# A spectral transformer block's gradient: who copies and stores the w2 gradient, four sets of gz tiles, and three moved pieces of matmul work

## The chip, the cores and the metric

The kernel runs on one core of one Trainium2 chip. The metric is the device time of one execution in microseconds; lower is better. The core's engines are TensorE (PE, matmuls), VectorE (DVE), ScalarE (ACT), GpSimd (POOL) and SyncE (SP, which here only asks for DMAs). Each engine works its own list of instructions in order and waits on semaphores for the others. DMAs are asked for by SyncE and GpSimd.

## The reference

The kernel computes the output and all gradients of one block (`jax.vjp`): 2048 tokens, D = 1024, F = 3584, everything bf16.

```python
mod = (_silu(c) @ w_mod).reshape(1, 6, 1, -1)        # six rows: sa, ca, ga, sb, cb, gb
h = _layernorm(x) * (1 + ca) + sa
x = x + ga * irfft2(rfft2(h) * (w_r + 1j * w_i))      # mixer A, over tokens and channels
h = _layernorm(x) * (1 + cb) + sb
y = _layernorm(h)
x = x + gb * (gelu(y @ w1 + b1) @ w2 + b2)            # mixer B
# and then, from grad_out: the gradients of x, w_r, w_i, w1, b1, w2, b2, c, w_mod
```

The outputs that matter below: `out_1` is the gradient of x, `out_2` and `out_3` those of `w_r` and `w_i`, `out_4` that of w1 (1024 x 3584), `out_6` that of w2 (3584 x 1024), `out_9` that of `w_mod`.

## The kernel before

One long program, not a loop: the language's scheduler orders each engine's list from the program's order, with some priorities (`tc.high_priority()`) and hand-written orders (`tc.issue_after(x)`: this comes behind x on its engine or by a semaphore). Tiles are named by tags; a tile with the tag of an older one lies in its place and waits until that one's last reader is done. PSUM has tags `f` (four accumulators of 128 x 512), `s` (two) and `d` (two).

The stages in order of time:

1. From 0 to some 125 us: the rows of modulation (`pm`, L278), and meanwhile the product of the output gradient with w2^T in blocks of 128 columns: `ph_part(fc, js)`, matmuls `pp` at L813, 8 for each of the four token quarters `js`. Blocks 0 to 5 (`PH_EARLY`) and the first two quarters of block 6 are written ahead of the first spectral part, the rest behind it.
2. The first spectral part (forward of mixer A): `s_fwd` (matmuls `pu`, L537, that read the folded input `fbuf`), channel transforms (`pcs`, L576), the product with `w_r + i w_i`, and back (`pv`, `po`).
3. The MLP forward (`pz`, L949), the output product (`pbo`, L1003), and the gradient with respect to its input: `pg_pass` (L1103), four passes b over the token quarters, each with two halves h of 7 w1^T groups g of 16 matmuls. Behind a pass of quarter b the column sums of quarter b - 1 (`sums3`, matmuls `acc3a` and `acc3b` at L217, that read `gn3a`, `gn3b`, `pru` and `au`, made by VectorE) are put among the groups: behind group 2, 3 and 4.
4. From some 944 us: the second spectral part (backward of mixer A), again `pu`, `pcs`, `pv` (L646, L662) and `po` (L748), with ScalarE copying V out of PSUM (L780). Its gaps on TensorE are filled by a generator, `pieces()`, called as `fill(n)`: n products of the w2 gradient (`gw2acc`, L1236, 16 matmuls each, one half row block of 128 x 512), and after all 56 of those the w1 gradient (`gw1acc`, L1454, 7 groups `fg` of 8 products).
5. The w2-gradient products are copied out by `gw2_out` (L1240 to L1247): into `gwo5` or `gwo[:, fc % 2]` (four halves that turn), by VectorE or ScalarE as the scheduler chooses (`nc.any`), and stored to `out_6`, all by GpSimd; from fc = 8 on half by half (L1245).
6. `consume_bwd(i, ...)`, i = 0 to 3, is the end of the second spectral part: VectorE unfolds a quarter of the result, does the layer norm backward, loads `xt` from `d_gx` (L1383, by SyncE), adds, stores `out_1`, and then TensorE sums columns (`accCA`, L217), with `fill((4, 6, 6, 8)[i])` ahead of that sum and `fill(3 if i == 1 else 2)` behind it.
7. Each w1-gradient group needs its 512 columns of `gz`, transposed on load from `d_gz` by SyncE (`gw1_load`, L1402), 1 MB in each of two tiles. Two sets of two tiles turn: group fg uses set fg % 2, and group fg + 1 is asked for ahead of group fg.
8. To the end, from some 1333 us: the rest of the w1 gradient, beside it rows 2, 1, 0 of the modulation gradient (`gmod_row`: loads `gr` and `wrw` by SyncE, VectorE's products, stores by GpSimd), ordered behind the last `gz` load that has been asked for.

The lists of SyncE and GpSimd matter here: SyncE has, in the stretch of stage 6, the `gz` loads, the `xt` loads and the `out_1` stores in one queue; GpSimd has the `out_6` and `out_9` stores, the stores of `out_2` and `out_3` and the spectral weights' loads in one.

Of the kernel before, what the change touches and what calls it, by code (L numbers as in the profile page):

```python
# [11 lines left out]
BF16 = mybir.dt.bfloat16  # L12
# [5 lines left out]
P = 128  # L18
# [5 lines left out]
NFC = F // P  # L24
# [6 lines left out]
NB = 4  # L31
# [4 lines left out]
def kernel(  # L36
# [24 lines left out]
    nc = tc.nc  # L61
    CE, CO, SE, SO = 0, 1, 2, 3
# [3 lines left out]
    reg = ctx.enter_context(tc.tile_pool(name="reg", bufs=1))  # L66
# [183 lines left out]
    c8, gb2r, b1r = (genv[0:n, 3136 + k * P:3136 + (k + 1) * P] for k, n in enumerate((NDC, NDC, NFC)))  # L250
# [94 lines left out]
    fbuf = reg.tile([P, 4, 4, D], BF16, name="fbuf", tag="fr")  # L345
# [177 lines left out]
    last_pu = [None]  # L523
    last_po = [None]

    def s_fwd(cl, fb, sm, evac):
        Ut = reg.tile([P, 8, 512], BF16, name=f"U{cl}", tag=f"uv{cl}")
        for c8 in range(8):
            pu = (ps_f if cl % 2 == 0 and c8 % 2 and fb is not fbuf else ps_s)("pu")
            for i in range(4 if cl % 2 else 0):  # L530
                last_pu[0] = nc.tensor.matmul(pu[:], lhsT=fb[:, i, cl, c8 * P:(c8 + 1) * P], rhs=sm[:, i, :],
                                              start=(i == 0), stop=(i == 3))
            for k in range(0 if cl % 2 else 2):
                cols = slice(k * 256, (k + 1) * 256)
                for j in range(2):
                    i = 2 * j + (k if cl == CE else 1 - k)
                    last_pu[0] = nc.tensor.matmul(pu[:, cols], lhsT=fb[:, i, cl, c8 * P:(c8 + 1) * P], rhs=sm[:, j, cols],  # L537
                                                  start=(j == 0), stop=(j == 1))
            with tc.high_priority():
                evac(Ut[:, c8, :], pu[:])  # L540
        return Ut
# [261 lines left out]
    last_pe = [None]  # L803
# [4 lines left out]
    def ph_part(fc, js):  # L808
        ph2 = phs[fc % 4]
        for j in js:  # L810
            pp = ps_f("pp")
            for cch in range(NDC):
                last_pe[0] = nc.tensor.matmul(pp[:], lhsT=wt[:, fc % 4, cch, :], rhs=gBoT[j][:, cch, :],  # L813
                                              start=(cch == 0), stop=(cch == NDC - 1))
            q = (0, 2, 3, 1)[j]
            ov = ph2[:, :, q * P:(q + 1) * P]
            pv = pp[:, :].rearrange("p (i w) -> p i w", w=P)
            with tc.high_priority():
                nc.any.tensor_copy(out=ov, in_=pv)  # L819
        if js[-1] == 3:  # L820
            nc.gpsimd.dma_start(out=d_ph[fc * P:(fc + 1) * P, :], in_=ph2.rearrange("p i w -> p (i w)"))
# [8 lines left out]
                for r, h in late_mods[3 * (fc // 2 - 1):3 * (fc // 2)]:  # L830
                    mod_block(r, h)

    ph_part(PH_EARLY, (0, 1))

    for i in range(4):
        x4, fb = x4s[i], fbuf[:, i]
# [55 lines left out]
            w1s.append(wtile)  # L892

    PH_KEEP = NFC - 4
    for fc in range(PH_EARLY, NFC):
        if fc >= PH_EARLY + 4:
            load_w2t(fc)
            load_w1({24: 1, 25: 1, 27: 5}.get(fc, 0))
        ph_part(fc, (0, 1) if fc >= PH_KEEP else (2, 3) if fc == PH_EARLY else (0, 1, 2, 3))

    hhA = reg.tile([P, 8, 4, BW], BF16, name="hhA", tag="fr")
    uvp0 = reg.tile([P, 2, 4, BW], BF16, name="hhB", tag="uv0")
# [194 lines left out]
    def pg_pass(b, h, pool, before=lambda: ExitStack()):  # L1097
        pgs = [pool(k)("pg") for k in range(4)]
        for g in range(7):
            for i in range(4):  # L1100
                for k in range(4):
                    with before():
                        last_pg[0] = nc.tensor.matmul(pgs[i][:], lhsT=gzs[b, g][:, k, i * P:(i + 1) * P],  # L1103
                                                      rhs=w1Ts[g][:, k, h * KH:(h + 1) * KH],
                                                      start=(g == 0 and k == 0), stop=(g == 6 and k == 3))
                    last_pe[0] = last_pg[0]
                if b > 0 and h == 0 and (g, i) in ((2, 0), (3, 2), (4, 2)):
                    for ins in sums_in[g - 2]:
                        behind(ins, last_pg[0])
                    sums_in[g - 2].clear()  # L1110
            for k in range(4 if b < 2 and h == 1 else 0):
                nc.scalar.activation(out=gzs[b, g][:, k, :], in_=gzs[b, g][:, k, :], func=ACT.Identity,  # L1112
                                     accum_out=gb1_acc[:, g * 4 + k, b:b + 1])
            if g < 6:
                yield
        for i in range(4):
            with tc.high_priority():
                nc.scalar.activation(out=gn3_of(b)[:, i, h * KH:(h + 1) * KH], in_=pgs[i][:], func=ACT.Identity,
                                     accum_out=g_sums[b][:, h, i:i + 1])
        yield  # L1120
# [118 lines left out]
    def gw2_out(acc, fc, h):  # L1239
        row = gwo5[fc % 5] if fc < 8 else gwo[:, fc % 2]  # L1240
        half = slice(h * KH, (h + 1) * KH)
        with tc.high_priority():
            nc.any.tensor_copy(out=row[:, half], in_=acc[:])  # L1243
        if fc >= 8:
            nc.gpsimd.dma_start(out=out_6[fc * P:(fc + 1) * P, half], in_=row[:, half])  # L1245
        elif h == 1:
            nc.gpsimd.dma_start(out=out_6[fc * P:(fc + 1) * P, :], in_=row)  # L1247

# [116 lines left out]
    def consume_bwd(i, o4, tmp, tmp2, n1, eb):  # L1365
        if i == 0:
            accCA.append(ps_s("accCA"))
            nc.vector.tensor_copy(out=sacc, in_=eb[:, 0, :])
        elif i == 2:
            tt(sacc, sacc, eb[:, 0, :], ALU.add)  # L1370
        unfold_d(o4, tmp)
        unfold_tok(o4, tmp)
        load_tok(n1, A_x, i, nc.gpsimd)
        with tc.issue_after(last_po[0].ins):
            norm_act(n1, n1, 0, i)
        tt(tmp, o4, n1, ALU.mult)
        s1c = small.tile([P, 4], FP32, tag="s1c")
        for q in range(4):
            t = 4 * i + q
            nc.vector.tensor_tensor_reduce(out=o4[:, q, :], in0=o4[:, q, :], in1=opca_row, scale=1.0, scalar=0.0,  # L1380
                                           op0=ALU.mult, op1=ALU.add, accum_out=s1c[:, q:q + 1])
            ln_bwd(o4[:, q, :], s1c[:, q:q + 1], n1[:, q, :], stats[:, 0, 0, t:t + 1], o4[:, q, :], tmp2[:, q, :])
        nc.sync.dma_start(out=n1, in_=chunk_rows(d_gx1, i))  # L1383
        tt(o4, o4, n1, ALU.add)
        store_tok(out_1, o4, i)
        fill((4, 6, 6, 8)[i])
        halves_sum(accCA[0], tmp, i == 0, i == 3)
        fill(3 if i == 1 else 2)
        if i == 3:
            rows = small.tile([P, D], BF16, tag="gmrow", bufs=1)  # L1390
            store_halves(accCA[0], rows[0:64, 0:KH], tmp, 1)


    w1g = {}

    def gw1_load(fg):
        for k in range(2):
            if fg == 0 and k == 0:
                nc.sync.dma_start(out=w1g["gz"][k][:].rearrange("p (j a) b -> p j (a b)", j=2),
                                  in_=d_gzT.rearrange("j p n -> p j n"))  # L1400
                continue
            ins = nc.sync.dma_start_transpose(out=w1g["gz"][2 * (fg % 2) + k][:],  # L1402
                                              in_=d_gz[fg * 512:(fg + 1) * 512, k * 1024:(k + 1) * 1024])
        return ins

# [5 lines left out]
    def pieces():  # L1411
# [25 lines left out]
        for b in range(NB):  # L1437
            n3n = reg.tile([P, 4, D], BF16, name=f"n3n{b}", tag=f"t{b}")
            nc.sync.dma_start(out=n3n[:], in_=chunk_rows(d_n3, b))
            n3ns.append(n3n)  # L1440
        w1g["gz"] = [reg.tile([P, 8, 512], BF16, name=f"gzh{k}", tag=f"px{(3, 4, 2, 5)[k]}") for k in range(4)]
        gwo1 = reg.tile([P, 8, 512], BF16, name="gwo1", tag="wt")
        w1g["wr"] = reg.tile([P, 4, D], BF16, name="wrw", tag="px1")
        w1g["gw"] = otl[:, 0:4 * D].rearrange("p (a d) -> p a d", d=D)
        w1g["gr"] = reg.tile([P, 2, D], BF16, name="gr", tag="sb")
        gw1_load(0)
        for fg in range(F // 512):
            if fg < 6:
                w1g["ins"] = gw1_load(fg + 1)
            gz2 = w1g["gz"][2 * (fg % 2):2 * (fg % 2) + 2]  # L1450
            for cch in range(NDC):
                acc = ps_f("gw1acc")
                for t in range(NT):
                    nc.tensor.matmul(acc[:], lhsT=n3ns[t // 4][:, t % 4, cch * P:(cch + 1) * P], rhs=gz2[t // 8][:, t % 8, :],  # L1454
                                     start=(t == 0), stop=(t == NT - 1))
                ob = gwo1[:, (fg * NDC + cch) % 8]
                with tc.high_priority():
                    nc.any.tensor_copy(out=ob, in_=acc[:])  # L1458
                eng = nc.sync if fg == 6 and cch > 4 else nc.gpsimd
                eng.dma_start(out=out_4[cch * P:(cch + 1) * P, fg * 512:(fg + 1) * 512], in_=ob)  # L1460
                yield
# [4 lines left out]
    def fill(n):  # L1466
        for _ in range(n):
            next(todo)
        done[0] += n
# [91 lines left out]
```

## Time and profile before

| | |
|---|---|
| runs (three) | 1413.61, 1414.35, 1414.64 us; median 1414.35 |
| profiled execution | 1423.68 us, its span 1421.8 us |
| granted TensorE clock, mean | 0.989 |
| TensorE busy | 1378.2 us (97%), 6963 matmuls |
| VectorE busy | 1071.2 us (75%) |
| ScalarE busy | 740.7 us (52%) |
| GpSimd busy | 374.7 us (26%) |
| DMA moved | 333.22 MB, mean 234 GB/s |

Rows of a timeline are: start, duration (both us), engine, line, operation, what it writes and reads, shapes, count; in brackets the idle time of the engine ahead of it and what ended it. Rows with x60 stand for a run of like instructions. SPq and POOL rows named DMA are the asking for a transfer, not the transfer. The times of a trace belong to the profiled execution, 9.3 us longer than the median of the runs. Rows of windows are: window, its length, busy time and count of PE, PEld, DVE, ACT and POOL, granted clock, share of the DMA engines' time, GB/s.

### The profile page before, as it was taken

How to read it: one execution, taken by the hardware profiler on the slowest of the kernel's cores; microseconds unless marked ns; L12 is line 12 of the kernel's file. 1: busy time of each engine (PE TensorE's matmuls, PEld its weight loads, DVE VectorE, ACT ScalarE, POOL GpSimd, SP SyncE). 2: the span in 40 equal slices, each digit the busy share in tenths (PEclk: the TensorE clock that was granted, in tenths of full speed). 3: DMA queues.
4: the chain of work that ended last, by engine and by line, in shares of the span. 5: the costliest groups of instructions: out<-in, count | busy, mean ns of one | idle time of the engine just before them, and what ended most of it. 6: DMA issues, size and time to landing. Idle time of an engine off the chain costs nothing. (4 is left out here: it accounts for less than half of the span.)

```text
span 1421.8 us, 18710 instructions
## 1 busy us (share of the span) xinstructions
PE 1378.2 (97%) x6963; PEld 665.5 (47%) x6963; DVE 1071.2 (75%) x1505; ACT 740.7 (52%) x1061; POOL 374.7 (26%) x476
## 2 busy tenths in 40 slices
PE   5898999999999999999999999999999999999998
PEld 2445575444444444444444444344545565444443
DVE  5897889987888877877520888999488658989733
ACT  4774657567877765666205574333632444343211
POOL 5600623201112112211110011012366431332322
PEclk8999999999999999999999999999999999999999
DMA  9972667899796876787999399995699997766796
GB/s 330 306 222 64 181 151 224 257 292 329 266 262 230 239 252 205 231 268 226 294 274 237 96 270 327 245 281 163 202 290 257 242 236 210 196 194 189 244 192 200
DMA packets 357426, 333.22 MB, mean 234 GB/s; under 512 B 208027, under 2 KB 298033, under 8 KB 357207
## 3 DMA queue, kind: packets, MB, share of 16 engines
q1 hardware_dynamic: 319990, 206.01, 56.7%
q0 software_dynamic: 37344, 126.03, 26.0%
q8 instruction: 54, 0.88, 0.3%
q14 instruction: 38, 0.30, 0.1%
HBM read 166.77 MB, written 115.92 MB: 199 GB/s over the span
## 5 line engine op out<-in xcount | busy, mean ns | idle before, releaser
L1454 PE MATMUL gw1acc<-gzh,n3n 128*128 128x512 bf16 x896 | 196.8, 381 | 4.5 <-DMA gzh<-d_gz 3.4
L813 PE MATMUL pp<-gBoT,wt 128*128 128x512 bf16 x896 | 197.9, 380 | 0.7 <-DVE phr L819 0.4
L1103 PE MATMUL pg<-w1T,gzr 128*128 128x512 bf16 x896 | 197.1, 381 | 0.0
L1454 PEld LDWEIGHTS <-n3n 128*128 128x128 bf16 x896 | 87.6, 98 | 111.4 <-issue 8.6
L1103 PEld LDWEIGHTS <-gzr 128*128 128x128 bf16 x896 | 86.9, 98 | 109.0 <-issue 7.0
L949 PEld LDWEIGHTS <-w 128*128 128x128 bf16 x896 | 87.3, 98 | 106.8 <-issue 2.5
L813 PEld LDWEIGHTS <-wt 128*128 128x128 bf16 x896 | 87.6, 98 | 103.7 <-issue 1.3
L949 PE MATMUL pz<-n3Tb,w 128*128 128x512 bf16 x448 | 99.2, 379 | 1.0 <-DVE w2sD L1025 1.0
L949 PE MATMUL pz<-n3Ta,w 128*128 128x512 bf16 x448 | 98.7, 379 | 0.0
L1003 PEld LDWEIGHTS <-hhA 128*128 128x128 bf16 x608 | 58.9, 98 | 74.2 <-issue 3.9
L1236 PE MATMUL gw2acc<-gB,hhsA 128*128 128x512 bf16 x416 | 92.4, 379 | 0.1
L952 ACT ACTIVATE gt<-pz,b_col 128x512 bf16<-128x512 f32 x112 | 72.8, 683 | 33.2 <-PE pz L949 32.9
L960 ACT ACTIVATE gt<-gt 128x2048 bf16<-128x2048 bf16 x28 | 53.5, 1910 | 64.9 <-DVE gt L194 64.9
L1243 ACT CAST gwo<-gw2acc 128x512 bf16<-128x512 f32 x47 | 27.2, 583 | 108.5 <-PE gw2acc L1236 60.9
L194 DVE TENSOR_TENSOR gt<-gt,gt 128x2048 bf16<-128x2048 bf16 x56 | 68.5, 1224 | 19.8 <-ACT gt L962 18.5
L194 DVE TENSOR_TENSOR ct<-ct 128x2048 bf16<-128x2048 bf16 x68 | 80.8, 1216 | 0.8
L1458 ACT CAST gwo<-gw1acc 128x512 bf16<-128x512 f32 x50 | 28.6, 581 | 96.9 <-PE gw1acc L1454 72.2
L1236 PEld LDWEIGHTS <-hhsA 128*128 128x128 bf16 x416 | 40.6, 98 | 47.8 <-DMA hhsA<-d_hh 0.6
L956 ACT ACTIVATE gt<-gt 128x2048 bf16<-128x2048 bf16 x28 | 53.5, 1910 | 2.1 <-DVE hhC L194 1.3
L962 ACT ACTIVATE gt<-gt 128x2048 bf16<-128x2048 bf16 x28 | 53.4, 1908 | 0.4
L1156 DVE CUSTOM_DVE_ANT_0 otl<-otl 128x1024 bf16<-128x1024 bf16 x24 | 28.9, 1219 | 28.8 <-DMA otl<-in_w_mod_dram 27.6
L1236 PE MATMUL gw2acc<-gB,otl 128*128 128x512 bf16 x224 | 50.0, 379 | 0.0
(347 smaller groups left out, 2528.4 us busy)
## 6 DMA issues: line engine op xcount, KB each, us to landing
gzr<-d_gz SPq DMA_DIRECT2D x28, 512.0 KB
wblk<-in_w_mod_dram SPq DMA_DIRECT2D x12, 1024.0 KB
out_dram<-otl POOLq DMA_DIRECT2D x48, 256.0 KB
out_dram<-gwo POOLq DMA_DIRECT2D x93, 128.0 KB
d_ph<-pho POOLq DMA_DIRECT2D x21, 512.0 KB
d_hh<-hhA POOLq DMA_DIRECT2D x19, 512.0 KB
w<-in_B_w_dram SPq DMA_DIRECT2D x7, 1024.0 KB
hhC<-d_ph SPq DMA_DIRECT2D x14, 512.0 KB
```

The costliest lines, as they stand in the source:

```text
L194: return nc.vector.tensor_tensor(out=out, in0=a, in1=b, op=op)
L813: last_pe[0] = nc.tensor.matmul(pp[:], lhsT=wt[:, fc % 4, cch, :], rhs=gBoT[j][:, cch, :], start=(cch == 0), stop=(cch == NDC - 1))
L949: last_pe[0] = nc.tensor.matmul(pz[:], lhsT=w1s[g][:, cch, k * P:(k + 1) * P], rhs=n3T[:, cch, :], start=(cch == 0), stop=(cch == NDC - 1))
L952: z_in = nc.scalar.activation(out=zb[:, k, :], in_=pz[:], func=ACT.Identity, bias=b1_col[:, fc:fc + 1], scale=1.0)
L956: nc.scalar.activation(out=av, in_=zb, func=ACT.Square)
L960: nc.scalar.activation(out=sg, in_=bv, func=ACT.Sigmoid, scale=2.0 * GK)
L962: nc.scalar.activation(out=bv, in_=bv, func=ACT.Sigmoid, scale=-2.0 * GK)
L1003: last_pe[0] = nc.tensor.matmul(pbs[i][:], lhsT=hh[:, k, i * P:(i + 1) * P], rhs=wp[:, k, :], start=False, stop=(g == 6 and k == 3))
L1103: last_pg[0] = nc.tensor.matmul(pgs[i][:], lhsT=gzs[b, g][:, k, i * P:(i + 1) * P], rhs=w1Ts[g][:, k, h * KH:(h + 1) * KH], start=(g == 0 ...
L1156: step_in.append(nc.vector.tensor_tensor_reduce(out=buf, in0=buf, in1=gr, scale=1.0, scalar=0.0, op0=ALU.mult, op1=ALU.add, accum_out=gu[: ...
L1236: nc.tensor.matmul(acc[:], lhsT=hh_of(fc)[:, t, :], rhs=gBs[t // 4][:, t % 4, h * KH:(h + 1) * KH], start=(t == 0), stop=(t == NT - 1))
L1454: nc.tensor.matmul(acc[:], lhsT=n3ns[t // 4][:, t % 4, cch * P:(cch + 1) * P], rhs=gz2[t // 8][:, t % 8, :], start=(t == 0), stop=(t == NT ...
```

## The change

Five things are changed:

- the second half of block 6 of the w2^T product is written ahead of the first spectral part, whose first two `pu` matmuls are ordered behind it;
- in the last `pg_pass` (b = 3) the column sums go behind groups 3, 4 and 5 and not 2, 3 and 4;
- in `consume_bwd`, for i = 1, seven products and not six are ahead of the column sum, and two and not three behind it;
- the `gz` tiles of the w1 gradient are four sets, not two, used as 0, 1, 0, 1, 2, 3, 0; sets 2 and 3 have the tags `uv0` to `uv3` of the spectral part's V tiles, and the loads of groups 4, 5 and 6 are all written at group 3;
- the w2-gradient rows from the ninth on (fc >= 8, 40 half rows) are copied by ScalarE and stored by a DMA that ScalarE asks for.

```diff
@@ s_fwd
-                    last_pu[0] = nc.tensor.matmul(pu[:, cols], ...)
+                    with tc.issue_after(early_pe.ins) if fb is fbuf and cl == CE else ExitStack():
+                        last_pu[0] = nc.tensor.matmul(pu[:, cols], ...)
...
-    ph_part(PH_EARLY, (0, 1))
+    ph_part(PH_EARLY, (0, 1, 2, 3))
+    early_pe = last_pe[0]
...
-    for fc in range(PH_EARLY, NFC):
+    for fc in range(PH_EARLY + 1, NFC):
...
-        ph_part(fc, (0, 1) if fc >= PH_KEEP else (2, 3) if fc == PH_EARLY else (0, 1, 2, 3))
+        ph_part(fc, (0, 1, 2, 3) if fc < PH_KEEP else (0, 1))
@@ pg_pass
-                if b > 0 and h == 0 and (g, i) in ((2, 0), (3, 2), (4, 2)):
-                    for ins in sums_in[g - 2]:
+                g0 = 3 if b == NB - 1 else 2
+                if b > 0 and h == 0 and (g, i) in ((g0, 0), (g0 + 1, 2), (g0 + 2, 2)):
+                    for ins in sums_in[g - g0]:
@@ gw2_out
-            nc.any.tensor_copy(out=row[:, half], in_=acc[:])
+            if fc >= 8:
+                nc.scalar.copy(out=row[:, half], in_=acc[:])
+                nc.scalar.dma_start(out=out_6[fc * P:(fc + 1) * P, half], in_=row[:, half])
+            else:
+                nc.any.tensor_copy(out=row[:, half], in_=acc[:])
         if fc >= 8:
-            nc.gpsimd.dma_start(out=out_6[fc * P:(fc + 1) * P, half], in_=row[:, half])
+            pass
@@ consume_bwd
-        fill((4, 6, 6, 8)[i])
+        fill((4, 7, 6, 8)[i])
         halves_sum(accCA[0], tmp, i == 0, i == 3)
-        fill(3 if i == 1 else 2)
+        fill(2)
@@ gw1_load
-            ins = nc.sync.dma_start_transpose(out=w1g["gz"][2 * (fg % 2) + k][:],
+            ins = nc.sync.dma_start_transpose(out=w1g["gz"][2 * w1g["set"][fg] + k][:],
@@ pieces
+        w1g["set"] = [0, 1, 0, 1, 2, 3, 0]
...
-            if fg < 6:
-                w1g["ins"] = gw1_load(fg + 1)
-            gz2 = w1g["gz"][2 * (fg % 2):2 * (fg % 2) + 2]
+            if fg == 3:
+                w1g["gz"] += [reg.tile([P, 8, 512], BF16, name=f"gzu{k}", tag=f"uv{k}") for k in range(4)]
+            for k in {0: (1,), 1: (2,), 2: (3,), 3: (4, 5, 6)}.get(fg, ()):
+                w1g["ins"] = gw1_load(k)
+            gz2 = w1g["gz"][2 * w1g["set"][fg]:2 * w1g["set"][fg] + 2]
```

More of the change, by code (lines that the diff above doesn't have):

```diff
@@ L536, in s_fwd @@
                     i = 2 * j + (k if cl == CE else 1 - k)
-                    last_pu[0] = nc.tensor.matmul(pu[:, cols], lhsT=fb[:, i, cl, c8 * P:(c8 + 1) * P], rhs=sm[:, j, cols],
+                    with tc.issue_after(early_pe.ins) if fb is fbuf and cl == CE else ExitStack():
+                        last_pu[0] = nc.tensor.matmul(pu[:, cols], lhsT=fb[:, i, cl, c8 * P:(c8 + 1) * P], rhs=sm[:, j, cols],
                                                   start=(j == 0), stop=(j == 1))
@@ L1106, in pg_pass @@
                     last_pe[0] = last_pg[0]
-                if b > 0 and h == 0 and (g, i) in ((2, 0), (3, 2), (4, 2)):
-                    for ins in sums_in[g - 2]:
+                g0 = 3 if b == NB - 1 else 2
+                if b > 0 and h == 0 and (g, i) in ((g0, 0), (g0 + 1, 2), (g0 + 2, 2)):
+                    for ins in sums_in[g - g0]:
                         behind(ins, last_pg[0])
-                    sums_in[g - 2].clear()
+                    sums_in[g - g0].clear()
             for k in range(4 if b < 2 and h == 1 else 0):
```

## The prediction, made before the changed kernel had run

> **What bounds the kernel now.** I read the page's first part, then the list of what TensorE waited for, then the timelines of the engines around each of those waits.
>
> ```profile
> span 1421.8 us, 18710 instructions
> PE 1378.2 (97%) x6963; PEld 665.5 (47%) x6963; DVE 1071.2 (75%) x1505; ACT 740.7 (52%) x1061; POOL 374.7 (26%) x476
> ```
>
> ```profile
> PE pu L537 <- DVE fbuf L194: 3.6, 1, 3.6
> PE gw1acc L1454 <- DMA gzh<-d_gz: 3.4, 1, 3.4
> PE acc3a L217 <- DVE gn3a L1201: 2.9, 2, 2.1
> PE pv L646 <- ACT V L780: 2.1, 1, 2.1
> PE accCA L217 <- DVE ct L194: 1.6, 1, 1.6
> ```
>
> TensorE (PE) is busy for 1378.2 of 1421.8 us, so the kernel is bound by its matmuls and only 1421.8 - 1378.2 = 43.6 us can be won without taking matmuls out. The change takes none out: it moves some. The rows of the second fence (waits in us: sum, times, longest) are single waits of 1.6 to 3.6 us, each beside a place that the change touches: 3.6 + 3.4 + 2.9 + 2.1 + 1.6 = 13.6 us. That is the pot. A wait is won only if what follows it comes earlier too, so each part below asks what is late next.
>
> **Part 1, the seventh w2^T block (block 6) whole ahead of the spectral part.** The diff moves its second half, 16 `pp` matmuls, and holds two early `pu` matmuls back.
>
> ```profile
> 104.71 13.11 PE L813 MATMUL pp<-gBoT,wt 128*128 128x512 bf16 x60
> 121.38 1.46 PE L537 MATMUL pu<-smA,fbuf 128*128 128x256 bf16 x6 [3.55 <-DVE fbuf L194]
> ```
>
> The scheduler had that half ahead of the wait already: before, 16 `pp`, two `pu`, 60 `pp`, then the wait; now 32 `pp`, two `pu`, 44 `pp`, then the same `pu`. 76 `pp` stand ahead of the wait both times and VectorE's order there is unchanged, so the 3.55 us stay. Part 1: 0; bounds from -0.4 to +0.4 (two `pu` of 0.2 us each).
>
> **Part 2, the column sums of the last pass one w1^T group later.** The sums waited twice; now 16 more `pg` matmuls of the same shape as the last row's stand ahead of them: 16 x 20.88/96 = 3.5 us.
>
> ```profile
> 897.85 0.39 PE L217 MATMUL acc3a<-gn3a,ones_bf 128*32 128x512 bf16 x2 [2.13 <-DVE gn3a L1201]
> 899.04 0.61 PE L217 MATMUL acc3a<-gn3a,ones_bf 128*32 128x512 bf16 x2 [0.81 <-DVE gn3a L1201]
> 959.27 2.28 DVE L194 TENSOR_TENSOR pru<-gn3b,n2u 128x4096 bf16<-128x4096 bf16 x1
> 964.68 0.39 PE L217 MATMUL acc3a<-pru,ones_bf 128*32 128x512 bf16 x2
> 991.96 2.48 DVE L194 TENSOR_TENSOR fbuf<-fbuf,gzr 128x2048 bf16<-128x2048 bf16 x2
> 1000.20 3.98 PE L537 MATMUL pu<-smf,fbuf 128*128 128x256 bf16 x35
> 1207.14 20.88 PE L1454 MATMUL gw1acc<-gzh,n3n 128*128 128x512 bf16 x96
> ```
>
> 2.13 + 0.81 = 2.94 us go, and 3.5 covers them. Late next: `pru` is ready at 959.27 + 2.28 = 961.55 and TensorE would come for it at 964.68 - 2.94 = 961.74, 0.2 us later; the spectral part needs `fbuf` of 994.44 at 1000.20 - 2.94 = 997.26. Both hold, the first narrowly. Part 2: -2.9; bounds -2.9 and -1 (VectorE's chain is not sped up, and could be a little later than here).
>
> **Part 3, one w1-gradient product more ahead of the second `accCA` sum.**
>
> ```profile
> 1227.32 2.29 DVE L194 TENSOR_TENSOR ct<-ct,xt 128x4096 bf16<-128x4096 bf16 x1
> 1229.66 0.62 PE L217 MATMUL accCA<-ct,ones_bf 128*32 128x512 bf16 x8 [1.64 <-DVE ct L194]
> ```
>
> One product is 16 matmuls, 3.5 us, against 1.64 us of wait. Part 3 by itself: -1.6. Whether it lasts is told at the next sum, below.
>
> **Part 4, four sets of `gz` tiles.** Loads of groups 4, 5 and 6 are asked for at group 3, sets 2 and 3 being put where the spectral part's V tiles lay.
>
> ```profile
> 1235.60 8.97 SPq L1402 DMA_TRANSPOSE gzh<-d_gz  x2
> 1245.53 0.36 SPq L1383 DMA_DIRECT2D xt<-d_gx  x1
> 1360.63 26.55 SPq L1402 DMA_TRANSPOSE gzh<-d_gz  x2
> 1390.74 27.49 PE L1454 MATMUL gw1acc<-gzh,n3n 128*128 128x512 bf16 x120 [3.36 <-DMA gzh<-d_gz]
> 1235.00:1333.00 98.00, 97.51 (x493) 46.62 (x492) 87.67 (x122) 38.52 (x50) 25.95 (x37) 1.00 0.69 195
> 1333.00:1422.00 89.00, 81.35 (x369) 36.20 (x368) 34.20 (x69) 15.41 (x28) 25.57 (x46) 0.98 0.89 211
> ```
>
> The last two transposed loads held SyncE for 26.55 us while the DMA engines were 0.89 busy (the last rows' last but one column), and TensorE waited 3.36 us for them. In the new order they lie before about 1310, in a stage 0.69 busy. The wait goes, and the gmod rows' loads move up behind them. Two waits for `gwo` stores in the same stretch (under 1 us each) I leave as they are. So -3.4.
>
> Its price lies on SyncE: a transposed load for the new tiles now stands ahead of each `xt` load, on which VectorE's chain hangs.
>
> ```profile
> 1251.90 2.29 DVE L194 TENSOR_TENSOR ct<-ct,xt 128x4096 bf16<-128x4096 bf16 x1 [3.91 <-DMA xt<-d_gx]
> 1269.18 2.29 DVE L194 TENSOR_TENSOR ct<-ct,xt 128x4096 bf16<-128x4096 bf16 x1
> 1273.54 0.62 PE L217 MATMUL accCA<-ct,ones_bf 128*32 128x512 bf16 x8
> 1304.39 2.29 DVE L194 TENSOR_TENSOR ct<-ct,xt 128x4096 bf16<-128x4096 bf16 x1
> 1310.99 0.61 PE L217 MATMUL accCA<-ct,ones_bf 128*32 128x512 bf16 x8
> ```
>
> At the third sum VectorE is done at 1269.18 + 2.29 = 1271.47 and TensorE comes at 1273.54: 2.07 us of slack, of which part 3 uses 1.64, so 0.4 is left. Two loads took 8.97 us, one 4.5. SyncE starts the pair 1.64 earlier (group 0's tiles come free by so much sooner), the third load follows, and `xt` is asked for at 1235.60 - 1.64 + 8.97 + 4.5 = 1247.4 where it was 1245.53: 1.9 later, and it shares the DMA engines with the load ahead of it. VectorE already waits for `xt` there (3.91 us), so the whole delay is seen: 1.9 - 0.4 = 1.5 at least, about 3.6 if sharing costs another 2. I take 2, near the lower end, as the stage is 0.69 busy. At the fourth sum the slack is 1310.99 - 1306.68 = 4.3 us, which covers as much again. Part 4: -3.4 + 2.0 = -1.4; bounds -3.4 and +0.2.
>
> **Part 5, w2-gradient rows from the ninth on by ScalarE.** Forty half rows of 128 KB are copied and now also stored by ScalarE (ACT) where GpSimd (POOL) stored them.
>
> ```profile
> L1460 SPq DMA_DIRECT2D out_dram<-gwo x3: 338/343/344, 1412.0 to 1419.1; - x3
> 1101.54 0.58 ACT L1243 CAST gwo<-gw2acc 128x512 bf16<-128x512 f32 x1 [2.50 <-PE pcs L576]
> 1107.78 0.58 POOL L1245 DMA_DIRECT2D out_dram<-gwo  x1 [2.41 <-DMA out_dram<-gwo]
> 1115.10 0.59 ACT L1243 CAST gwo<-gw2acc 128x512 bf16<-128x512 f32 x1 [5.58 <-DMA out_dram<-gwo]
> 1119.88 6.30 PE L646 MATMUL pv<-smf,R 128*128 128x256 bf16 x41 [2.08 <-ACT V L780]
> ```
>
> Four halves of `gwo` turn. What was copied at 1101.54 was asked to be stored only at 1107.78, GpSimd being behind its own waits, so the copy of 1115.10 into that half came 5.58 us late, the V copies behind it too, and TensorE lost 2.08. With the store right behind the copy some 5.7 us of this go (1107.78 - 1102.12), more than the 2.08. The issues cost ScalarE between 40 x 0.34 = 14 us (the same kind of store asked for by SyncE) and 40 x 0.58 = 23 us (by GpSimd); I take the first, as its row is the plainer one. ScalarE is 48% idle and each copy has a product of 3.5 us beside it, which hides either; without that cover the store ahead of a V copy costs its 0.3 to 0.6 us. GpSimd's queue loses 40 issues, so its spectral loads and stores come earlier; nothing waits for them on TensorE's list, and I count no gain. [...] Part 5: -1.5; bounds -2.1 and the slower rival below.
>
> **The sum.** 0 - 2.9 - 1.6 - 1.4 - 1.5 = -7.4; 0.2 back for `pru`: -7.2 us. The profiled execution took 1423.7 us (span 1421.8) and would take 1416.5; the runs' median, 1414.35, lies 9.3 below it at the same work, so I take the same difference off it: 1407.1 us. A measurement of this kernel tells about 0.2% (2.8 us) from no change.
>
> **The rivals.**
>
> *ScalarE stands behind SyncE's transposed loads (slower).* No DMA of before is asked for by ScalarE, so nothing shows what such an issue costs while SyncE is inside one of its long ones.
>
> ```profile
> 1157.91 14.14 PE L662 MATMUL pv<-smB,R 128*128 128x256 bf16 x128
> 1158.15 0.58 ACT L1243 CAST gwo<-gw2acc 128x512 bf16<-128x512 f32 x1 [2.87 <-PE gw2acc L1236]
> 1159.31 15.97 SPq L1416 DMA_TRANSPOSE otl<-d_hh  x1
> 1198.04 14.72 SPq L1402 DMA_TRANSPOSE gzh<-d_gz  x3
> 1203.98 2.25 ACT L1243 CAST gwo<-gw2acc 128x512 bf16<-128x512 f32 x4
> 1206.12 1.08 ACT L753 CAST ct<-po 128x512 bf16<-128x512 f32 x2
> ```
>
> If the two take turns at one thing, two places are on the path. The store behind the copy of 1158.15 would be asked for at 1158.73, 0.6 us ahead of a load that holds SyncE for 15.97; all 16 V copies follow that store on ScalarE and `pv` has two accumulators (14.14/8, some 1.8 us), so if it falls behind the load TensorE loses up to 15.97 - 1.8 = 14 us. And four stores now stand between the copies of 1203.98 and those of `po` at 1206.12, inside three transposed loads that end at 1212.76: up to 6.6 us on VectorE's chain to the second sum, where part 3 left 3.5 - 1.6 = 1.9 of room: +4.7. Stores elsewhere meet shorter loads, and four `gw2acc` accumulators of 3.5 us each stand between. With the second place alone: -7.2 + 4.7 = -2.5, 1411.8. With both: -7.2 + 4.7 + 14 = +11.5, 1425.8; half of the first place, +4.5, 1418.9. It decides against the change once these stalls pass 7.2 us. For it: the sheer length of the loads. Against it: the order at 1158.73, and that many such loads are waits for something else.
>
> [...]
>
> *Nothing is given back at the third sum.* The load for the new tiles does not delay `xt`, as SyncE is free early enough, and part 5 gives all: -2.9 - 1.6 - 3.4 - 2.1 = -10.0, 1404.3. For it: VectorE's next wait there (a `ct` store) may hide some of the delay.
>
> *More is given back.* Sharing costs 2 more at the third sum and part 5 nothing: -7.2 + 1.6 + 1.5 = -4.1, 1410.3.
>
> *The parts do not do what they say.* The scheduler or the tiles' release keeps sets 2 and 3 late, so that the end wait stays and only SyncE's price is paid, and part 3 is eaten: -2.9 - 1.6 + 2.0 + 0.2 = -2.3, 1412.0: no change that can be told. Part 1 is such a case already.
>
> **How the numbers follow.** The forecast 0.36; nothing given back 0.16; more given back 0.12; does not do what it says, or the second place alone, 0.11; ScalarE held so that it ends slower 0.25. Faster by over 0.2% (under 1411.5): 0.36 + 0.16 + 0.12 = 0.64; within 0.2%: 0.11; slower (over 1417.2): 0.25. The range: from 1403.5, a little under the case with nothing given back, to 1421.5, which takes in the half-paid stall of 1418.9 and leaves out the full one: some 0.18 outside. The faster cases alone lie between 1403.5 and 1411.
>
> **What would show it.** Right: in the new profile the waits of `acc3a`, the late `gw1acc` and `pv` L646 are gone from TensorE's list, `pu` keeps 3.6, and `accCA` has moved its wait to the third sum with some 2 us; ScalarE's stores take some 0.34 us each. Wrong: such stores lasting as long as SyncE's load beside them, V or `po` copies late behind them, TensorE waiting on `pv` L662 or `accCA` for over 3 us; or the end wait still there.

## The result

| | before | changed |
|---|---|---|
| median of 22 runs each | 1416.39 us (1411.97 to 1422.71) | 1413.01 us (1409.56 to 1417.18) |
| profiled execution, span | 1423.68, 1421.8 us | 1412.42, 1410.6 us |

The ratio is 0.9974, 95% interval 0.9963 to 0.9986: some 3.5 us faster, where 7.2 were forecast. On a second chip (12 runs against 35) the medians were 1411.47 and 1414.08, ratio 0.9986 (0.9971 to 1.0002), and in a third comparison 1412.25 and 1414.00, 0.9979 (0.9962 to 0.9997).

The two profiled executions differ by 11.2 us, three times as much as the medians. The first profile of before was slower than all 22 of its runs in the comparison; that is the first thing to keep in mind below.

The changed kernel's page and the largest and the telling rows of TensorE's waits:

```profile
span 1410.6 us, 18696 instructions
PE 1374.2 (97%) x6963; PEld 664.5 (47%) x6963; DVE 1072.4 (76%) x1507; ACT 739.2 (52%) x1059; POOL 351.2 (25%) x436
```

```profile
PE pu L538 <- DVE fbuf L194: 5.1, 1, 5.1
PE pg L1105 <- ACT gn3b L1121: 2.8, 1, 2.8
...
PE accCA L217 <- DVE ct L194: 1.6, 1, 1.6
...
PE gw1acc L1464 <- ACT gwo L1468: 1.2, 1, 1.2
```

Idle time of TensorE: 1421.8 - 1378.2 = 43.6 us before, 1410.6 - 1374.2 = 36.4 after. By chance that is the 7.2 us of the forecast, but made up otherwise. The other 4.0 us are busy time, though the matmuls are the same 6963: 43.6 us was not all that could be won, since time at a lower clock (below) counts as busy: 41 `pv` matmuls took 6.30 us behind the V wait, at a mean granted clock of 0.73, 128 of the same shape 14.14 us at 1.00 (both rows are in the prediction's fifth part and its rivals). The waits on `gn3a`, on V and on `gzh` at the end are gone; a new one on ScalarE's copies of `gn3b` has come, the one of `accCA` has moved from the second sum to the third, and one on `gwo` copies has grown (0.8 us before).

**The sums.** First TensorE's, then ScalarE's timeline, changed kernel:

```profile
909.24 6.22 PE L1105 MATMUL pg<-w1T,gzr 128*128 128x512 bf16 x28
918.30 7.07 PE L1105 MATMUL pg<-w1T,gzr 128*128 128x512 bf16 x32 [2.84 <-ACT gn3b L1121]
```

```profile
916.43 1.24 ACT L1203 ACTIVATE got<-n2u,sc 128x1024 bf16<-128x1024 bf16 x1 [3.76 <-DVE sc L1202]
917.58 0.58 ACT L1121 ACTIVATE gn3b<-pg 128x512 bf16<-128x512 f32 x1
```

The second half of the pass needs the accumulators of the first. ScalarE copies them only behind a `got` that waits 3.76 us for VectorE. TensorE came earlier and waited 2.84 us there: the 2.94 us of the two waits before were handed on to the next place that hangs on VectorE's chain.

**The gz sets.** SyncE, VectorE and TensorE around the third sum, changed kernel; the row behind them is before's wait for the same `ct` store, and the last is the changed kernel's window of the stage that takes the loads in:

```profile
1227.47 8.72 SPq L1409 DMA_TRANSPOSE gzh<-d_gz  x2
1236.31 3.92 SPq L1409 DMA_TRANSPOSE gzu<-d_gz  x1
1240.34 0.51 SPq L1390 DMA_DIRECT2D xt<-d_gx  x1
1241.28 7.71 SPq L1409 DMA_TRANSPOSE gzu<-d_gz  x1
1249.09 0.51 SPq L164 DMA_DIRECT2D out_dram<-ct  x1
```

```profile
1246.74 2.29 DVE L194 TENSOR_TENSOR ct<-ct,xt 128x4096 bf16<-128x4096 bf16 x1 [4.59 <-DMA xt<-d_gx]
...
1255.75 1.23 DVE L194 TENSOR_TENSOR ct<-eb 128x2048 bf16<-128x2048 bf16 x1 [3.65 <-DMA out_dram<-ct,xu]
```

```profile
1267.07 0.61 PE L217 MATMUL accCA<-ct,ones_bf 128*32 128x512 bf16 x8 [1.59 <-DVE ct L194]
```

```profile
1258.41 1.23 DVE L194 TENSOR_TENSOR ct<-eb 128x2048 bf16<-128x2048 bf16 x1 [2.48 <-DMA out_dram<-ct,xu]
```

```profile
1235.00:1333.00 98.00, 94.98 (x474) 44.73 (x472) 85.90 (x120) 36.21 (x48) 25.85 (x39) 1.00 0.93 238
```

Two loads for the new tiles, 3.92 and 7.71 us, surround the second `xt` load; VectorE waits 4.59 us for `xt` (3.91 before) and 3.65 for the `ct` store (2.48 before), and TensorE 1.59 where 2.0 had been taken. The share of the DMA engines' time in this stage, 0.69 before (in the prediction's fourth part), is 0.93 with the loads in it.

**ScalarE's stores.** All forty in one row, then a transposed load of SyncE's and a store inside it:

```profile
L1248 ACTq DMA_DIRECT2D out_dram<-gwo x40: 338/338/375, 1025.9 to 1200.1; - x40
```

```profile
1195.72 4.25 SPq L1409 DMA_TRANSPOSE gzh<-d_gz  x1
```

```profile
1197.51 0.34 ACTq L1248 DMA_DIRECT2D out_dram<-gwo  x1
```

No store took longer than 0.375 us, also where it lay wholly inside one transposed load, as here (0.34 us inside 4.25). The slower rival does not happen.

**The clock.** Windows of 4 us, the third number from the end is the granted clock; three of before's waits (`gn3a`, V, `gzh`) and, last two rows, the new wait of the changed kernel:

```profile
896.00:900.00 4.00, 1.35 (x6) 0.34 (x6) 4.00 (x4) 1.51 (x2) 0.68 (x2) 0.84 1.10 238
900.00:904.00 4.00, 4.00 (x15) 1.64 (x14) 2.93 (x9) 2.37 (x2) 0.47 (x1) 0.73 0.94 291
1116.00:1120.00 4.00, 1.92 (x19) 1.57 (x17) 3.93 (x7) 1.24 (x3) 0.79 (x2) 1.00 0.91 261
1120.00:1124.00 4.00, 4.00 (x23) 3.00 (x22) 4.00 (x5) 3.67 (x8) 3.43 (x4) 0.58 1.15 268
...
1388.00:1392.00 4.00, 1.26 (x4) 0.43 (x4) 0.00 (x0) 0.00 (x0) 0.00 (x0) 0.78 1.07 223
1392.00:1396.00 4.00, 4.00 (x16) 1.63 (x15) 3.17 (x6) 0.58 (x1) 2.21 (x4) 0.79 0.76 286
```

```profile
916.00:920.00 4.00, 1.70 (x8) 0.78 (x8) 3.96 (x11) 3.54 (x9) 0.53 (x1) 1.00 1.02 377
920.00:924.00 4.00, 4.00 (x20) 1.85 (x19) 2.60 (x4) 1.24 (x1) 0.00 (x0) 1.00 0.31 50
```

Behind the V wait of 2.08 us the clock was 0.58 for 4 us: 0.42 x 4 = 1.7 us more, nearly as much as the wait. Beside the `gn3a` waits it was (0.16 + 0.27) x 4 = 1.7 us, behind the end wait (0.22 + 0.21) x 4 = 1.7 us. Behind the new wait of 2.84 us it stayed at 1.00. Such a dip is the second part of a wait's price, and it comes in one execution and not in another: in the second profile of the changed kernel the third sum's wait of 2.0 us had one (0.57), in its third the wait on `gn3b` (2.98 us; 0.60 from 916 to 920, where it ends).

### The profile page after: what moved, and what is told of

Its sections match the earlier page's. It is cut to its first block, busy times and chain, and to the rows that moved or that the text cites. A ratio compares the mean times of both kernels' runs of the same rounds, so it can differ in the third digit from the quotient of the medians.

```text
span 1410.6 us, 18696 instructions
## 1 busy us (share of the span) xinstructions
PE 1374.2 (97%) x6963; PEld 664.5 (47%) x6963; DVE 1072.4 (76%) x1507; ACT 739.2 (52%) x1059; POOL 351.2 (25%) x436
## 5 line engine op out<-in xcount | busy, mean ns | idle before, releaser
L1464 PE MATMUL gw1acc<-gzh,n3n 128*128 128x512 bf16 x640 | 140.0, 379 | 0.2 <-DVE gwo L1468 0.2
L1247 ACT CAST gwo<-gw2acc 128x512 bf16<-128x512 f32 x40 | 23.3, 584 | 93.6 <-PE gw2acc L1239 90.5
L1470 POOL DMA_DIRECT2D out_dram<-gwo x53 | 29.2, 554 | 129.8 <-DVE gwo L1468 67.6
L1464 PE MATMUL gw1acc<-gzu,n3n 128*128 128x512 bf16 x256 | 55.6, 379 | 1.2 <-ACT gwo L1468 1.2
```

## The experiments

All ratios are to the kernel before, beside it on the same chip, 12 runs against 35, with a 95% interval behind each. The kernel before, compared with itself so, gave medians 1.25 us apart, so that a difference of about 1 us says nothing. The first four ran on one chip together.

### The changed kernel again

> The changed kernel once more, beside the kernel before, for a second profile and a yardstick for the next three. Theory 1 (three parts do nothing lasting: the first, the sums one group later and the product ahead of the second accCA sum; the four sets of gz tiles and ScalarE's stores carry the gain): ratio to the kernel before 0.996 to 0.998, and the new profile again has the pg wait on ACT gn3b (2 to 3 us) and the accCA wait (1 to 2 us). Theory 2 (the profile was not typical: these two waits are accidents of one execution and the sums' 2.9 us are won in most runs): the same ratio, but the two waits are mostly gone from this profile.

Measured: 1411.47 us, 0.9986 (0.9971 to 1.0002). Its profile again has the wait on `gn3b` (2.8 us) and that of the third sum (2.0). They are no accidents. That the sets carry a part of the gain, which the first theory held too, does not last (below).

### The sums as before

```diff
-                g0 = 3 if b == NB - 1 else 2
+                g0 = 2
```

> The changed kernel with the column sums of the last pass back behind groups 2, 3 and 4. Theory 1 (ACT's copies of gn3b, behind VectorE's chain, take the time back at once): no slower than the changed kernel by more than 1 us; the acc3a waits of 2 to 3 us are back and the pg wait on ACT gn3b is gone or under 1 us. Theory 2 (the gain of 2.9 us is real in most runs): 2.5 to 3 us slower than the changed kernel, about 1415.7 beside its 1413.0.

Measured: 1411.13 us, 0.9978 (0.9961 to 0.9996): 0.3 us beside the changed kernel's 1411.47. TensorE's rows of this run:

```profile
895.51 0.39 PE L217 MATMUL acc3a<-gn3a,ones_bf 128*32 128x512 bf16 x2 [1.64 <-DVE gn3a L1203]
...
909.08 21.11 PE L1105 MATMUL pg<-w1T,gzr 128*128 128x512 bf16 x97
```

The `acc3a` waits are back (1.64 and 0.80 us), and the 97 `pg` matmuls behind them run without the wait on `gn3b`. Theory 1 holds: this part wins nothing that these runs can tell.

### Two gz sets

```diff
-        w1g["set"] = [0, 1, 0, 1, 2, 3, 0]
+        w1g["set"] = [0, 1, 0, 1, 0, 1, 0]     # and group fg + 1 asked for ahead of group fg, as before
```

> The changed kernel with two sets of gz tiles, as before. Theory 1: the end wait on gzh of 3 to 3.5 us is back, the accCA wait of 1.6 us at the third sum is gone (no transposed load ahead of xt), so 1.5 to 3 us slower than the changed kernel. Theory 2 (the wait at the third sum is an accident): 3 to 3.5 us slower, as the end wait is all there is.

Measured: 1410.81 us, 0.9971 (0.9953 to 0.9989), 0.7 us less than the changed kernel. Both theories fall: taking the two new sets away costs nothing. The end wait is back in this profile

```profile
1381.21 19.15 PE L1461 MATMUL gw1acc<-gzh,n3n 128*128 128x512 bf16 x88 [3.05 <-DMA gzh<-d_gz]
```

(with 0.93 us ahead of it, 4.0 in all), but the waits at the third sum and on `gwo` at 1327 are gone.

### The stores by GpSimd

```diff
-            if fc >= 8:
-                nc.scalar.copy(out=row[:, half], in_=acc[:])
-                nc.scalar.dma_start(out=out_6[...], in_=row[:, half])
-            else:
-                nc.any.tensor_copy(out=row[:, half], in_=acc[:])
+            nc.any.tensor_copy(out=row[:, half], in_=acc[:])
         if fc >= 8:
-            pass
+            nc.gpsimd.dma_start(out=out_6[...], in_=row[:, half])
```

> The changed kernel with the w2-gradient half rows from the ninth on copied by whichever engine the scheduler takes and stored by GpSimd, as before. Theory 1: ACT's waits on the gwo stores (16 us in the trace of before) and TensorE's pv wait of 2.1 us are back: 1.5 to 2.1 us slower than the changed kernel. Rival (the late stores only filled ScalarE's idle time, and the 2.1 us is an accident of the DMA traffic in one execution): within 0.7 us of the changed kernel.

Measured: 1416.39 us, 1.0017 (1.0000 to 1.0035): 4.9 us more than the changed kernel, and slower than before. That is more than either theory had, and in this profile neither the `pv` wait is there nor ScalarE's waits for `gwo` stores in the second spectral part (16.4 us before). What is there, SyncE, VectorE and TensorE:

```profile
1241.40 12.88 SPq L1405 DMA_TRANSPOSE gzu<-d_gz  x2
1254.38 0.54 SPq L164 DMA_DIRECT2D out_dram<-ct  x1
```

```profile
1262.43 1.23 DVE L194 TENSOR_TENSOR ct<-eb 128x2048 bf16<-128x2048 bf16 x1 [8.02 <-DMA out_dram<-ct]
```

```profile
1264.31 8.75 PE L1460 MATMUL gw1acc<-gzh,n3n 128*128 128x512 bf16 x32 [2.81 <-DVE gwo L1464]
```

Without ScalarE's stores the scheduler puts both new loads behind the second `xt` load, 12.88 us ahead of the `ct` store; VectorE waits 8.02 us for that store, and its next work, a `gwo` copy, is what TensorE waits for. So this run does not price the stores alone; the next ones do.

### The kernel before again, and each of the two larger parts alone

> The kernel before once more, for a second profile. If its first profile is typical: PE's pv wait on ACT V (2.1 us), ACT's four waits on gwo stores from 1098 to 1119 and the end wait on gzh of 3 to 3.5 us are all there again and the profiled execution is 7 us or more above the median. If it was not: the profiled execution is within 3 us of the median of 1414, the pv wait and ACT's waits on the gwo stores are gone or under 1 us, the acc3a waits are followed by up to 1 us on ACT gn3b, and of the waits that the change removes only the end wait stays.

Measured: 1413.60 us, 0.9995 (0.9977 to 1.0012) to itself; profiled execution 1416.15. The end wait is there (4.0 us), the `pv` wait is not, though ScalarE again waited 18.1 us for `gwo` stores. The first profile was not typical: it had every wait on its list, and a dip of the clock behind three of them.

The first is the kernel before with the fifth part alone, the second with the fourth alone:

> The kernel before with ScalarE's copies and stores alone. If ScalarE's stores carry the gain: 2 to 4 us faster than before, 1410 to 1412, as fast as the whole change, and runs that lie as close together as those of the changed kernel (1409 to 1415) and not as far apart as before's (1408 to 1420). Rival (their 5 us in the changed kernel came only from where the scheduler puts the new gz loads, so that alone they are worth nothing): within 1 us of before.

Measured: 1409.28 us, 0.9964 (0.9951 to 0.9977), all 12 runs from 1407.16 to 1411.83, where the 12 of before again lie from 1408.76 to 1419.48. ScalarE's stores alone win at least as much as the whole change did on its chips (0.9974, 0.9986, 0.9979); the intervals overlap.

> The kernel before with four sets of gz tiles alone. The order of SyncE's list has here two transposed loads between the third xt load and the ct store, as in the run with GpSimd's stores. If that order costs what the end wait gave: within 2 us of before or slower by up to 2 us, with the end wait gone and a wait of 2.5 to 4 us in all at the third accCA sum and the gwo copies ahead of it. Rival (the end wait of 3.4 us is won): 3 us faster than before, about 1411.

Measured: 1415.16 us, 1.0016 (1.0002 to 1.0030). Alone the four sets win nothing and are slower, if barely clear of the noise. The end wait is gone, but `gwo` copies (1.20 us) and the third sum (2.38) wait, 3.6 us in all, as the first theory had it. Here too ScalarE does not wait for `gwo` stores in the second spectral part, although GpSimd asks for them.

### The new sets later

```diff
-                w1g["ins"] = gw1_load(k)
+                with tc.issue_after(w1g["st"].ins) if k in (4, 5) else ExitStack():   # "st": the third ct store
+                    w1g["ins"] = gw1_load(k)
```

> The changed kernel with the loads into the two new sets ordered behind the third ct store, which the scheduler turns into: behind the fourth. No transposed load for them then stands ahead of the third or fourth xt load. If these loads cause the wait at the third sum: it is gone (1.6 to 2.0 us in the two profiles of the changed kernel), the end wait stays gone, and it is 1.5 to 2.8 us faster than the changed kernel, 1409 to 1410. Rival (VectorE is late at the third sum by itself since the seven products shortened its time): the wait stays at 1 us or more and the time is that of the changed kernel, 1411.5.

Measured: 1420.27 us, 1.0043 (1.0027 to 1.0060). Slower than before by 6 to 8 us, far from both. The expectation misread the list: the loads stand ahead of the fourth `xt` load, six in a row.

```profile
1296.60 23.04 SPq L1413 DMA_TRANSPOSE gzu<-d_gz  x4
1319.73 9.98 SPq L1413 DMA_TRANSPOSE gzh<-d_gz  x2
1329.83 0.52 SPq L1392 DMA_DIRECT2D xt<-d_gx  x1
```

```profile
1338.93 1.06 ACT L1526 ACTIVATE sr<-accSA 1x512 f32<-1x512 f32 x2 [18.11 <-DVE ct L196]
```

```profile
1340.51 4.71 PE L1469 MATMUL gw1acc<-gzu,n3n 128*128 128x512 bf16 x15 [8.96 <-ACT gwo L1473]
```

The wait at the third sum is gone, so the loads were its cause. And the run shows a second chain that the forecast lacks: VectorE adds `xt` for the fourth time, ScalarE's `sr` waits for VectorE, four `gwo` copies stand behind `sr` on ScalarE, and TensorE runs out of accumulators. Whatever stands ahead of the fourth `xt` load on SyncE is paid there.

### Copies alone, and stores by SyncE

The kernel before with `nc.scalar.copy`, and the store once by `nc.gpsimd.dma_start`, once by `nc.sync.dma_start`.

> The kernel before with ScalarE's copies of the w2-gradient half rows from the ninth on, but GpSimd's stores: the copying half of the fifth part alone. If the gain of 3 to 4 us of that part comes from where the stores are asked for: within 1 us of before, ACT's waits on gwo stores of some 16 us are there and the runs lie as far apart as before's (10 us). If it comes from the copies or from the order that the scheduler makes of them: 3 to 4 us faster, 1409 to 1410.

Measured: 1414.69 us beside 1416.74, 0.9982 (0.9958 to 1.0006): not told from no change. Its profile has the V wait of the first profile, with ScalarE's waits for the stores (17.8 us) and the dip of the clock:

```profile
1115.48 6.91 PE L646 MATMUL pv<-smf,R 128*128 128x256 bf16 x48 [2.43 <-ACT V L780]
```

```profile
ACT gwo L1244 <- DMA out_dram<-gwo: 17.8, 5, 5.2
```

```profile
1116.00:1120.00 4.00, 4.00 (x27) 3.01 (x26) 4.00 (x7) 3.62 (x8) 3.69 (x4) 0.67 1.13 221
```

> The kernel before with ScalarE's copies and the stores asked for by SyncE. If all that counts is that the stores leave GpSimd's list: as fast as with ScalarE asking, 3 to 4 us faster than before. If the asking engine must be one that is free at once: SyncE's transposed loads of 2 to 16 us hold the stores up, ACT waits for gwo stores again and V copies come late, 1 us faster to 5 us slower than before.

Measured: 1416.67 us beside 1416.74, 1.0007 (0.9989 to 1.0025). Leaving GpSimd's list is not enough: SyncE's transposed load holds the store back, and the V wait comes.

```profile
1106.47 4.77 SPq L1420 DMA_TRANSPOSE otl<-d_hh  x1
1111.34 0.53 SPq L1245 DMA_DIRECT2D out_dram<-gwo  x1
```

```profile
1113.65 0.59 ACT L1244 CAST gwo<-gw2acc 128x512 bf16<-128x512 f32 x1 [5.49 <-DMA out_dram<-gwo]
```

```profile
1114.78 7.08 PE L646 MATMUL pv<-smf,R 128*128 128x256 bf16 x48 [2.08 <-ACT V L780]
```

So who asks matters here: on SyncE 4.77 us of a load stood ahead of this store, where ScalarE asked for its forty in the changed kernel in 0.338 to 0.375 us each, also inside such loads. That the copies by ScalarE carry none of the gain is not shown: the interval of the copies alone (0.9958 to 1.0006) overlaps that of ScalarE's stores (0.9951 to 0.9977). The stores by SyncE are clear of them, also on this chip: 1416.67 us against 1410.87 with ScalarE asking and the seven products (next).

### Without the sets, the sums and block 6; and one set more, late

The first keeps ScalarE's stores and the seven products only. The second has besides a third set for group 6 alone, its loads ordered behind the fourth `xt` load:

```diff
+        w1g["set"] = [0, 1, 0, 1, 0, 1, 2]
...
-            if fg < 6:
-                w1g["ins"] = gw1_load(fg + 1)
+            for k in {4: (5, 6), 5: (), 6: ()}.get(fg, (fg + 1,)):
+                with tc.issue_after(w1g["xt"].ins) if k == 6 else ExitStack():   # "xt": the fourth xt load
+                    w1g["ins"] = gw1_load(k)
```

> The kernel before with ScalarE's copies and stores and the seven products ahead of the second accCA sum, without the other three parts. If the parts add up by their waits: the accCA wait of 0.7 us that ScalarE's stores left is gone, no wait comes at the third sum as no new gz load stands ahead of an xt load, and it is 0 to 1 us faster than the stores alone: 4 to 5 us faster than before. Rival: the later work is late by as much and it equals the stores alone.

Measured: 1410.87 us beside 1416.74, 0.9957 (0.9933 to 0.9981), not told from the stores alone (0.9964). The profile has no wait at the second or third sum.

> The same with one more gz set in place of two, used for the last group alone, its loads ordered behind the fourth xt load. If a new set costs only where its loads stand ahead of an xt load, and wins the end wait: no end wait on gzh, no wait over 1 us at the third and fourth sum, and no slower than the run beside it without the set; up to 2 us faster if that one has an end wait in most of its runs. Rival (the loads hold up what follows them on SyncE there, the ct store and the gmod rows): a wait of 1 us or more on gwo copies after 1320, and 1 to 4 us slower than the run beside it.

Measured: 1413.48 us beside 1416.74, 0.9977 (0.9956 to 0.9998). Its end wait is gone, but group 5's tiles come late instead:

```profile
1354.75 10.48 PE L1462 MATMUL gw1acc<-gzh,n3n 128*128 128x512 bf16 x40 [2.17 <-DMA gzh<-d_gz]
```

The loads moved ahead push those behind them: SyncE is in the two for the new set for 6.48 and 10.32 us, and only then, at 1337.04, comes to group 5's two, which take 15.66. It costs by the medians 2.6 us; the intervals overlap.

### On one chip: the changed kernel, the short version, a later third sum, block 6

> The changed kernel again, as the yardstick on the same chip for the next three: 2.5 to 4 us faster than before.

Measured: 1412.25 us, 0.9979 (0.9962 to 0.9997).

> ScalarE's copies and stores and the seven products, without the other three parts, beside the changed kernel. If the four gz sets give back what they win and the sums win nothing: 0.5 to 2.5 us faster than the changed kernel. Rival (the whole is at least as good, the first run of this kernel was lucky): equal within 0.5 us or slower.

Measured: 1408.66 us, 0.9969 (0.9951 to 0.9987), 3.6 us less than the changed kernel by the medians; the intervals of the two ratios overlap. In its profile TensorE waits nowhere for more than 0.3 us from 902 on; of the five waits of the forecast's pot only these two are left:

```profile
PE pu L537 <- DVE fbuf L194: 4.1, 1, 4.1
...
PE acc3a L217 <- DVE gn3a L1201: 2.5, 3, 1.5
```

```diff
-        fill((4, 7, 6, 8)[i])
+        fill((4, 7, 7, 8)[i])
         halves_sum(accCA[0], tmp, i == 0, i == 3)
-        fill(2)
+        fill(1 if i == 2 else 2)
```

> The changed kernel with seven products, not six, also ahead of the third accCA sum and one, not two, behind it. If the wait at the third sum is what the new gz loads ahead of the second xt load cost: that wait (1.6 and 2.0 us in two profiles) is gone and it is 1.5 to 2 us faster than the changed kernel, up to 3.5 where that wait had halved the clock behind it as in the second profile. Rival (something later, as the gwo copies at 1327 behind ScalarE's sr, takes it): that wait grows from 1.2 to over 2 us and the time stays.

Measured: 1415.00 us, 0.9997 (0.9980 to 1.0013), 2.75 us more than the changed kernel by the medians: the rival, and perhaps more. The wait at the third sum is gone, and the chain through `sr` takes it:

```profile
1296.91 14.06 SPq L1409 DMA_TRANSPOSE gzh<-d_gz  x2
...
1318.88 0.39 SPq L1390 DMA_DIRECT2D xt<-d_gx  x1
```

```profile
1329.45 1.06 ACT L1521 ACTIVATE sr<-accSA 1x512 f32<-1x512 f32 x2 [10.89 <-DVE ct L194]
```

```profile
1331.03 14.15 PE L1464 MATMUL gw1acc<-gzu,n3n 128*128 128x512 bf16 x57 [3.44 <-ACT gwo L1468]
```

```profile
1332.00:1336.00 4.00, 4.00 (x13) 1.45 (x11) 4.00 (x10) 0.41 (x1) 2.51 (x5) 0.57 0.97 335
```

3.44 us where the changed kernel has 1.20, and 0.43 x 4 = 1.7 us of clock behind it.

> The changed kernel with block 6 of the w2^T product split as before. If the first part changes nothing, as the order of the matmuls says: within 1 us of the changed kernel, the pu wait on fbuf 3 to 5 us. Rival (the two early pu products that it moves matter): over 1 us away.

Measured: 1412.39 us, 0.9983 (0.9966 to 1.0000), 0.1 us from the changed kernel; the `pu` wait is 4.1 us. The first part is worth nothing, as the order said.

## Why the prediction was wrong

The direction held, the size did not: -7.2 us forecast, some -3.5 measured. Two steps failed, part 2 (-2.9, measured 0) and part 4 (-1.4, measured nothing or a loss), and part 5 won more than its term. In size the result is near the rival *More is given back* (-4.1), but that is luck: its condition, that part 5 gives nothing, is the opposite of what the runs show. By its own steps:

- **Part 1, 0 us.** Right (last run).
- **Part 2, -2.9 us.** Wrong: 0 (0.3 us between the kernels with and without it). The step "late next" looked at `pru` and `fbuf` and passed over ScalarE's copies of `gn3b`, which hang on VectorE's chain and took back 2.84 us within 20 us. The lower bound, -1, was still too good. A dip of the clock comes with either wait: beside `gn3b` in six of the eight profiles that have the sums moved (0.60, 0.67 and 0.68 over 4 us in the last three), beside `gn3a` in four of the ten that have not (0.73 in before's first, 0.70 with one set more).
- **Part 3, -1.6 us.** Its wait at the second sum goes. With the sets it comes back at the third, as foreseen. Without them the two runs gave 0.9957 and 0.9969 against 0.9964 for the stores alone: no gain that these runs can tell.
- **Part 4, -1.4 us, the step that failed worst.** The end wait goes, and the third sum costs 0.9 to 2.0 us in the three profiles of the changed kernel, as priced. But the -3.4 us are not there to be won in each execution: with ScalarE's stores and two sets the end wait was 0, 0, 1.7 and 4.0 us in four profiles. And the stage that takes the loads in did not stay 0.69 busy, it went to 0.93. Alone the sets are 0.02 to 0.30% slower; taking them out with parts 1 and 2, which are worth nothing, won 3.6 us by the medians. Why they cost more than the waits in the profiles add up to is not shown. The step at the fourth sum was also short: I saw 4.3 us of slack and stopped there. Behind it stands the chain from the fourth `xt` load over VectorE, `sr` and the `gwo` copies to TensorE. In the changed kernel it costs little (1.20 us in one profile, nothing in the other two, 0.8 and 0.2 before), but what is put ahead of that load is paid there: 3.44 us with the third sum later, 8.96 with the new sets later.
- **Part 5, -1.5 us.** Mis-sized: 0.36% (0.23 to 0.49%) alone, 3 to 7 us. Its mechanism is right as far as it goes. The V wait is there in three of the six profiles without ScalarE's stores (before's first, copies alone, stores by SyncE) and in none of the twelve with them. It is 2.1 to 2.4 us of wait and some 1.7 of clock around its end, so some 4 us in those three executions and nothing in the others. What else the stores win, and by which wait, is open. The sum counts 1.5 of the V wait's 2.1 us; the 0.6 us between them no run shows: in the twelve profiles with ScalarE's stores the wait was gone whole.
- **The clock.** No term of the sum had it. It fell behind V waits of 2.08 us (before's first profile, 0.58 over 4 us) and 2.43 us (copies alone, 0.67), and not behind a wait of 2.84 us (changed kernel, 1.00).
- **From the profile to the median.** I took one difference for all. The first profile of before was slower than the 22 runs beside it and held the V wait, the end wait and three dips together; the second, 7.5 us shorter, had no V wait. What a change removes from such a profile is not in most runs.
- **The slower rival** fell: in the changed kernel's profile no store that ScalarE asked for took longer beside SyncE's load (0.363 us at most inside one, 0.375 of all forty).

Net, as an estimate from the ratios: 0 + 0 + 0 for the first three parts, some -3 to -5 us for the stores, some +1 to +3 for the sets. Open: how often the end wait and the dips come in executions without a profile, which only the spread of the runs hints at.

The best version is the short one, stores and seven products: 0.9957 and 0.9969 in two comparisons, and 3.6 us below the changed kernel beside it by the medians. Without the seven products it is not told from that.

## What to carry to other kernels

A wait that goes is won only up to the next place that hangs on the same slow engine (here a wait of 2.84 us came for the 2.94 us that went); follow that engine's chain through every engine that copies for it before counting. Let the engine that made the data ask for its store, if it is otherwise idle: what counted here was what stands ahead in the asking engine's list (1416.67 us with SyncE asking, 1410.87 with ScalarE and the seven products), and the same holds for a new load put ahead of one that somebody waits for (TensorE waited 8.96 us with six loads ahead of the fourth `xt` load). And take a second profile before believing a list of waits of 2 us (before's second was 7.5 us shorter and had no V wait).

## What was not expected of the hardware

- Behind before's V wait of 2.08 us TensorE's clock was 0.58 over 4 us, 1.7 us lost (in windows of 1 us: 0.80 from 1120, 0.50 in each of the three from 1121 to 1124, 0.99 from 1124); behind the changed kernel's wait of 2.84 us it stayed at 1.00.
- Forty stores asked for by ScalarE took 0.338 to 0.375 us each. Fourteen of them lay wholly inside one transposed load of SyncE's (1.2 to 6.2 us long) and took no longer than 0.363 us.
- Runs of before lie 10 to 19 us apart (1408.89 to 1419.32 and 1410.76 to 1429.83, 35 runs each in two comparisons). The 4.7 us of the 12 runs with ScalarE's stores alone is no mark of those stores: with the seven products the 12 runs lie 8.1 and 9.3 us apart, and with four sets and GpSimd's stores 4.4.
